# Delta-rule attention with a GELU feed-forward: the row steps of the block inversion move from VectorE to GpSimd

## The chip, the cores and the metric

The kernel runs on one core of a Trainium2 chip. The metric is the time of one execution in microseconds of the device; all times here are from runs of the kernel before the change. A core has five engines that run beside each other, each with its own queue in program order: TensorE (PE, with its weight loads PEld), VectorE (DVE), ScalarE (ACT), GpSimd (POOL) and SyncE (SP, here only for issuing DMAs).

## What is computed

Inputs are q, k, v of shape (4, 8, 768, 48), beta of shape (4, 8, 768), and two weight matrices of 384 x 2048 and 2048 x 384, all in float32.

```python
k_n = k / (norm(k) + 1e-06)
for t in range(768):                       # for each of 32 heads
    y[t] = q[t] @ state
    v_old = k_n[t] @ state
    state = state + beta[t] * outer(k_n[t], v[t] - v_old)
x = y, as 3072 tokens of 384               # (batch, time) x (head, dim)
h = x @ w_in
out = (0.5 * h * (1 + erf(h / sqrt(2)))) @ w_out
```

## The kernel before

**Attention.** The 768 steps are cut into 12 chunks of 64. A chunk of two of the four batches is a unit (`tiles[c, a]`, a = 0, 1). Inside a chunk the recurrence is a triangular system of 64 x 64 for each head. Two chunks make a group g (0 to 5) with 64 systems. Each system is split into blocks of 32: the two diagonal blocks are inverted by elimination, and the off-diagonal block is put together by two levels of small matmuls, the joins.

The parts of a group that the change touches, with their lines:

- `norms`, `prep`, `finish` (L338 to L362): sums of squares of k on ScalarE and VectorE (L354), a power on GpSimd (L356), and the factors on VectorE (L306 to L310).
- `eliminate_steps(g)` (L475): `scales` transposes the factors (L481, VectorE) and spreads them over a triangle (L486, GpSimd); `flip` transposes the diagonal blocks into `Nu`, 128 partitions x 32 x 32 (L491); `scaled_flip` multiplies by the factors (L496). Then 30 row steps follow, each needing the one before: step j multiplies column j by row j into `tmp` (L510) and adds it to the rows below (L512), (31 - j) x j elements of each partition; j = 1 and j = 30 are one instruction (L505). `diagonal` (L516) writes ones. `back` transposes the result into `XM` (L521) and `Zf` (L525); a third copy within `Zf` is ScalarE's (L529). All the rest of the list is VectorE's.
- `join_steps(g)` makes three runs of joins (L602): level 0 of the first chunk; level 1 of the first with level 0 of the second; level 1 of the second. Level 0 is evicted by VectorE (L614), level 1 by ScalarE through `put_off` and `copy_out` (L581).
- `state_steps(c)`: keys and queries against the state (L676, subtracted at L687), the solve (L711), outputs and the state's update (L741, L752; read at L757 and L767), and the turning of the outputs into tokens (L803).
- `scale_v` (L381) on GpSimd scales each V as it arrives.

**Feed-forward.** Each layer is multiplied by seven products in place of eight. From chunk 4 on, the layers run over pairs of chunks. The first layer is four blocks (`part_of_layer`, L943) of eleven products; each product is two matmuls of 256 columns. VectorE first forms four differences of the tokens (`mix_x`, L908), then reads each block's PSUM at L971, L1002 (`add_p5`), L979 and L991. The second layer (`two`, L877; `read2`, L1045 to L1056) has seven products of eight matmuls for each chunk. The products of the feed-forward stand in one fixed line (`behind`).

**What sets the order.** Every step is put in a list `plan` with a position in units of chunks: `at(first, last, steps)` spreads steps between two positions, `emit` sorts all and issues them. A pair's first layer begins at w - 1 and its two layers end at w + 1, where w is the even chunk whose attention runs meanwhile. VectorE runs in the order of the plan; ScalarE has some orders kept (`keep`), TensorE some runs (`together`, `behind`), and a scheduler orders the rest, GpSimd and SP included. `rows_of(g, w, pieces)` puts the elimination's list in the plan piece by piece, each piece a number of steps with its first and last position. Before, the row steps of groups 3 to 5 are spread from w - 1.03 to w - 0.245, between VectorE's reads for the first layer.

Of the kernel before, what the change touches and what calls it, by code (L numbers as in the profile page):

```python
# [19 lines left out]
def kernel(  # L20
# [150 lines left out]
    G = Gp[0]  # L171
    spare = Gp[1].rearrange("q a f n -> q (a f n)")
    low = spare[:, 0:HB * HB].rearrange("q (a b) -> q a b", b=HB)
    early_sq = spare[:, HB * HB:HB * HB + H * D].rearrange("q (h d) -> q h d", d=D)
    nc.gpsimd.memset(mask, 1.0)
    nc.gpsimd.memset(low, 1.0)
    nc.gpsimd.affine_select(out=low, in_=low, compare_op=ALU.is_ge, fill=0.0, base=-1,
# [134 lines left out]
    def squares(u, n, engine=None):  # L312
        kd = u.Kn[:, :, 0:D]
        if engine is nc.gpsimd:
            ksq = su.tile([128, H, D], F32, tag="w_e", name="ksq")
        elif engine is None:
            if u.a == 0:
                ns["ksq"] = more[0].tile([128, NA, H, D], F32, tag="TX", name="ksq")
            u.ksq = ns["ksq"][:, u.a]
            keep(nc.scalar.activation, u.ksq, kd, ACT.Square)  # L320
            return
        else:
            ksq = early_sq
        engine.tensor_tensor(ksq, kd, kd, op=ALU.mult)
        nc.vector.tensor_reduce(n, ksq, axis=AX.X, op=ALU.add)
# [148 lines left out]

    def eliminate_steps(g):  # L475
        steps = []

        def scales():
            gt = wk.tile([128, HB], F32, tag="gt", name="gt", bufs=1)
# [13 lines left out]
                scaled_flip()  # L493

        def scaled_flip():
            nc.vector.tensor_tensor(Nus[g], Nus[g], XMs[g], op=ALU.mult)  # L496

        def eliminate(j):
            nu = Nus[g]
            n = HB - 1 - j  # L500
            if j == 1 or n == 1:
                to = (slice(2, HB), slice(0, 1)) if j == 1 else (slice(HB - 1, HB), slice(0, j))
                by = (slice(2, HB), slice(1, 2)) if j == 1 else (slice(j, j + 1), slice(0, j))
                factor = nu[:, 1, 0:1] if j == 1 else nu[:, j + 1, j:j + 1]
                nc.vector.scalar_tensor_tensor(nu[:, to[0], to[1]], nu[:, by[0], by[1]], factor,  # L505
                                               nu[:, to[0], to[1]], ALU.mult, ALU.add)
                return
            tmp = wk.tile([128, HB * HB // 4], F32, tag="tmp", name="tmp", bufs=1)
            tmp = tmp[:, 0:n * j].rearrange("q (i c) -> q i c", i=n)
            nc.vector.tensor_tensor(tmp, nu[:, j + 1:, j:j + 1].to_broadcast([128, n, j]),  # L510
                                    nu[:, j:j + 1, 0:j].to_broadcast([128, n, j]), op=ALU.mult)
            nc.vector.tensor_tensor(nu[:, j + 1:, 0:j], nu[:, j + 1:, 0:j], tmp, op=ALU.add)  # L512

        def diagonal():
            flat = Nus[g].rearrange("q i c -> q (i c)")
            nc.vector.memset(flat[:, 0:HB * HB:HB + 1], 1.0)  # L516

        def back(x):
            nu = Nus[g]
# [56 lines left out]
    def put_off(name, dst, src):  # L576
        copies[name].append((dst, src))
# [6 lines left out]
    def join_run(g, ts0, ts1):  # L584
# [21 lines left out]
        for level, u0, psJ in sets:  # L606
            for p in range(2):
                for e in range(2):
                    us = slice(u0 + e, u0 + 2 * H, 2)
                    at_ = p * C + e * HB  # L610
                    src = psJ[at_:at_ + HB, :, e * HB:(e + 1) * HB]
                    if level == 0:
                        low_ = slice(p * C + HB, (p + 1) * C)
                        nc.vector.tensor_tensor(  # L614
                            xm[low_, us, :], src,
                            gm[low_, us].unsqueeze(2).to_broadcast([HB, H, HB]), op=ALU.mult)
                    else:
                        put_off("join", zf[p * C:p * C + HB, us, HB:C], src)
# [28 lines left out]
    def join_steps(g):  # L647
        a, b = range(NA), range(NA, 2 * NA)
        return [(join_run, g, a, ()), (join_run, g, b, a), (join_run, g, (), b)]
# [440 lines left out]
    def at(first, last, steps):  # L1090

        total, done, timed = sum(s[0] for s in steps), 0.0, []
        for w, *step in steps:
            timed.append((first + (last - first) * (done + 0.5 * w) / total, step))
            done += w
        return timed
# [164 lines left out]
    for c in range(4, NC):  # L1261
        us = [tiles[c, a] for a in range(NA)]
        even = c % 2 == 0
        for name, src, t in (("Kb", k, {4: 1.8, 5: 2.73, 6: 3.25}.get(c, c - (2.8 if even else 3.45))),
                             ("Qb", q, {4: 3.2, 5: 3.9}.get(c, c - (1.2 if even else 1.24)))):
            plan += [at(t, t + 0.01, [(1.0, load_blocks, c, name, src)])]
        for name, t in (("Kn", {4: 2.1, 5: 2.74, 7: 4.57}.get(c, c - (2.1 if even else 2.62))),
                        ("Kp", {4: 3.6, 5: 4.3}.get(c, c - (0.6 if even else 0.8)))):
            plan += [at(t, t + 0.01, [(1.0, load_k, c, name)])]
        t = {4: 2.7262, 5: 2.955, 7: 4.43}.get(c, c - (2.5 if even else 2.92))  # L1270
        plan += [at(t, t + 0.0005, [(1.0, turned_k, u) for u in us])]
        t = {4: 3.88, 5: 4.45}.get(c, c - (0.25 if even else 0.9))
        plan += [at(t, t + 0.01, [(1.0, turned_q, u) for u in us])]
    def gram(c):
        return [(grams, [tiles[c, a] for a in range(NA)])] if c < NC else []
# [16 lines left out]
    def second(c, t):  # L1292

        return [at(t + x, t + x + 0.001, steps) for x, steps in (
            (0.2, [(1.0, mix, c, 3, h) for h in range(2)]), (0.42, [(1.0, read_x, c)]))]

    for c in (2, 3, *range(4, NC, 2)):
        n = FH // blocks(c)
# [7 lines left out]
        else:  # L1306
# [2 lines left out]

    plan += [at(3.19, 3.191, [(1.0, transposed, u, (1,)) for u in fourth]),  # L1310
             at(3.1, 3.101, [(1.0, together, *gram(5))]),
             at(2.93, 2.931, [(1.0, norms, 5)]), at(2.95, 2.951, [(1.0, prep, 5)]),
             at(3.11, 3.111, [(1.0, finish, 4)]),
             state_at(3, 3.367, 3.59, 3.72, 3.93, second=query(3))]
    plan += rows_of(2, 3, ((1, 0.112, 0.113), (2, 0.16, 0.2), (4, 0.224, 0.31),
                           (2, 0.325, 0.365), (1, 0.395, 0.4), (2, 0.485, 0.5),
                           (2, 0.508, 0.54), (5, 0.6, 0.685), (7, 0.76, 0.88),
                           (3, 1.0, 1.05), (5, 1.07, 1.1), (1, 1.153, 1.154),
                           (1, 1.2, 1.201), (1, 1.201, 1.202)))
    for w in range(4, NC, 2):  # L1320
        more_to_come = w + 2 < NC
        if w == 4:
            begins = 0.25, 0.33, 0.41, 0.51, 0.6, 0.66, 0.7, 0.78, 0.87, 0.945
            n6, p6, n7, p7 = 0.53, 0.56, 0.75, 0.8
        else:
            begins = -0.22, -0.1, 0.02, 0.14, 0.27, 0.38, 0.42, 0.6, 0.76, 0.93
            n6, p6, n7, p7 = 0.3, 0.34, 0.56, 0.58
            plan += rows_of(w // 2, w, ((1, *((-1.19, -1.189) if w > 6 else (-1.05, -1.049))),
                                        (1, *((-1.18, -1.179) if w > 6 else (-1.04, -1.039))),
                                        (1, -1.035, -1.034), (4, -1.03, -1.0),  # L1330
                                        (3, -1.0, -0.95), (3, -0.935, -0.855), (2, -0.843, -0.785), (1, -0.77, -0.75),
                                        (3, -0.742, -0.692), (3, -0.677, -0.597), (2, -0.585, -0.527), (1, -0.512, -0.5),
                                        (3, -0.484, -0.434), (3, -0.419, -0.339), (2, -0.327, -0.269),
                                        (2, -0.255, -0.245), (2, -0.24, -0.23)))
        begins = [w + t for t in begins]
        j0, j1, j2 = join_steps(w // 2)
        plan += [at(begins[0], begins[0] + 0.001, [(1.0, together, j0, *query(w))]),
                 at(begins[1], begins[1] + 0.001, [(1.0, together, j1, *gram(w + 2))]),
                 state_at(w, *begins[2:6], second=[j2] + gram(w + 3)),
                 state_at(w + 1, *begins[6:], second=query(w + 1))]  # L1340
        plan += spread("join", 4, begins[1] + 0.025)
        plan += spread("join", 4, begins[3] + 0.02)
        if more_to_come:
            plan += spread("gram", 2, begins[1] + 0.01) + spread("gram", 2, begins[1] + 0.05)
            plan += spread("gram", 4, begins[3] + 0.04)
            plan += [at(w + n6, w + n6 + 0.001, [(1.0, norms, w + 2)]), at(w + p6, w + p6 + 0.001, [(1.0, prep, w + 2)]),
                     at(w + n7, w + n7 + 0.001, [(1.0, norms, w + 3)]), at(w + p7, w + p7 + 0.001, [(1.0, prep, w + 3)]),
                     at(w + p7 + 0.04, w + p7 + 0.041, [(1.0, finish, w + 2)])]
# [32 lines left out]
```

## Time and profile before

| what | us |
|---|---|
| median of 3 runs | 672.28 (671.87 to 673.04) |
| the profiled execution | 671.28 |
| its span, first to last instruction | 669.5 |
| mean granted TensorE clock in it | 0.962 |
| VectorE, L512 + L510 (168 each) | 59.0 + 56.9 |
| GpSimd, power L356 (10) | 30.8 |
| GpSimd, scaling of V L381 (18) | 15.4 |
| first layer of chunks 6 and 7 begins | 388.82 |
| first layer of chunks 8 and 9 begins | 491.29 |

An instruction's line in a timeline gives its start, its length, the engine, the line in the code, what it writes and reads, and in brackets how long the engine was idle ahead of it and who ended that. A line of the waits gives the engine and line that waited, for whom, the total, how often and the longest. "x4" behind a matmul row counts matmuls and weight loads together. Matmuls overlap, so the spacing of their starts tells more than their lengths.

### The profile page before, as it was taken

To read this page: it belongs to the slowest core of one execution; us is meant where nothing else is said; L and a number is where in the kernel's file an instruction comes from. 1 tells how busy PE (TensorE), PEld (TensorE's weight loads), DVE (VectorE), ACT (ScalarE), POOL (GpSimd) and SP (SyncE) were. 2 spreads that over 40 slices of the span, in tenths; PEclk is the share of its full clock that TensorE was granted. 3 is DMA by queue.
4 is the path that set the end of the run, shared out by engine and by line. 5 is a ranking of instruction groups with operands and counts; after the bars stand their busy time and mean duration, and the time that the engine had idled before them with its cause. 6 is when DMAs were issued, how large, how long until landed. Compare 5 with 4: busy or idle time off the path is not lost.

```text
span 669.5 us, 20804 instructions
## 1 busy us (share of the span) xinstructions
PE 621.9 (93%) x8998; PEld 551.8 (82%) x8998; DVE 490.1 (73%) x991; ACT 258.6 (39%) x584; POOL 68.1 (10%) x62
## 2 busy tenths in 40 slices
PE   5778999998998999869899989899989899999997
PEld 4667877766998899858799978799978799998997
DVE  7999989997779975689856689866689866333431
ACT  3576778333530365214461124362114441133300
POOL 4053002002200001300001310001210000000000
PEclk9578999999899999979999989999999999999999
DMA  9886682104333404431214520305120100010010
GB/s 130 176 254 181 105 222 63 24 12 80 49 60 46 72 10 72 80 60 18 32 23 82 90 49 12 38 14 98 31 55 0 25 4 14 14 24 1 0 25 24
DMA packets 158429, 39.70 MB, mean 59 GB/s; under 512 B 150017, under 2 KB 153217, under 8 KB 158337
## 3 DMA queue, kind: packets, MB, share of 16 engines
q1 hardware_dynamic: 155664, 37.34, 29.1%
q10 hardware_dynamic: 2672, 1.03, 0.8%
q8 instruction: 70, 1.15, 0.7%
q14 instruction: 23, 0.18, 0.1%
HBM read 33.62 MB, written 4.72 MB: 57 GB/s over the span
## 4 chain that ended last, share of the span: by engine, by line
PE 62%; DVE 25%; issue 6%; ACT 3%; DMA 1%; POOL 1%; SPq 0%; DVEq 0%; ACTq 0%; POOLq 0%
PE psX L877 10%; PE psY L943 8%; PE psY L877 7%; PE psX L943 5%; PE psV L943 4%; DVE tmp L510 4%; DVE Nu L512 4%; PE psG L419 4%; PE psV L877 3%; PE psZ L877 3%; PE psZ L943 3%; PE psO L844 2%; PE psK L676 2%; PE psH L826 2%; PE psT L398 2%
## 5 line engine op out<-in xcount | busy, mean ns | idle before, releaser
L943 PE MATMUL psX<-xT,w_in_sb 128*128 128x256 f32 (+1 forms) x288 | 63.7, 349 | 4.4 <-ACT pu L926 3.2
L512 DVE TENSOR_TENSOR Nu<-Nu,tmp 128x58 f32<-128x58 f32 (+13 forms) x168 | 59.0, 351 | 5.8
L510 DVE TENSOR_TENSOR tmp<-Nu 128x58 f32<-128x58 f32 (+13 forms) x168 | 56.9, 339 | 4.6
L356 POOL TENSOR_TENSOR n<-n,half 128x16 f32<-128x16 f32 x10 | 30.8, 3076 | 281.9 <-DVE n L354 232.1
L943 PEld LDWEIGHTS psX<-xT,w_in_sb 128*128 128x128 f32 x288 | 47.4, 191 | 11.0 <-ACT pu L926 4.4
L877 PE MATMUL psX<-w_out_sb,G 128*128 128x192 f32 x320 | 56.3, 329 | 0.0
L943 PE MATMUL psY<-xT,w_in_sb 128*128 128x256 f32 (+1 forms) x192 | 44.2, 361 | 10.9 <-DVE pu L1002 10.9
L877 PEld LDWEIGHTS psX<-w_out_sb,G 128*128 128x128 f32 x320 | 52.1, 190 | 0.5
L943 PEld LDWEIGHTS psY<-xT,w_in_sb 128*128 128x128 f32 x192 | 32.7, 196 | 16.2 <-DVE pu L1002 12.9
L826 PE MATMUL psH<-xT,w_in_sb 128*128 128x256 f32 x192 | 44.1, 383 | 1.5 <-ACT G L926 1.4
L844 PE MATMUL psO<-w_out_sb,G 128*128 128x384 f32 x128 | 43.9, 490 | 0.0
L826 PEld LDWEIGHTS psH<-xT,w_in_sb 128*128 128x128 f32 x192 | 35.8, 190 | 8.3 <-ACT G L926 2.3
L926 ACT COPY pu<-psZ 128x512 f32<-128x512 f32 x40 | 23.5, 586 | 45.2 <-PE psZ L943 23.2
L926 ACT COPY xT<-psX 128x768 f32<-128x768 f32 x9 | 7.2, 799 | 85.3 <-PE psX L803 85.3
L926 ACT ACTIVATE G<-G 128x512 f32<-128x512 f32 x40 | 25.2, 630 | 26.9 <-DVE G L979 26.5
L844 PEld LDWEIGHTS psO<-w_out_sb,G 128*128 128x128 f32 x128 | 23.6, 190 | 14.0
L1015 DVE TENSOR_TENSOR G<-G 128x512 f32<-128x512 f32 x20 | 13.6, 690 | 25.7 <-PE psX L877 25.7
L877 PE MATMUL psY<-w_out_sb,G 128*128 128x192 f32 x160 | 27.9, 327 | 2.0 <-DVE o_sb L1045 2.0
L877 PE MATMUL psV<-w_out_sb,G 128*128 128x192 f32 x160 | 28.0, 328 | 1.1 <-ACT y L688 1.1
L877 PE MATMUL psZ<-T,pu 128*128 128x192 f32 x160 | 28.4, 330 | 0.0
L877 PE MATMUL psY<-T,G 128*128 128x192 f32 x160 | 28.3, 329 | 0.0
L877 PE MATMUL psX<-T,G 128*128 128x192 f32 x160 | 28.1, 329 | 0.0
(186 smaller groups left out, 1316.8 us busy)
## 6 DMA issues: line engine op xcount, KB each, us to landing
Kp<-in_k_dram SPq DMA_DIRECT2D x76, 96.0 KB, 3.2
w_out_sb<-in_moe_w_in_dram SPq DMA_DIRECT2D x24, 256.0 KB, 4.1
w_raw<-in_moe_w_out_dram SPq DMA_DIRECT2D x16, 384.0 KB, 4.9
V<-in_v_dram SPq DMA_DIRECT2D x48, 96.0 KB, 3.2
out_dram<-o_sb SPq DMA_DIRECT2D x40, 96.0 KB, 2.2
Qp<-in_k_dram SPq DMA_DIRECT2D x64, 32.0 KB, 2.3
Qp<-in_q_dram SPq DMA_DIRECT2D x64, 32.0 KB, 2.3
Qp<-in_q_dram SPq DMA_DIRECT2D x16, 96.0 KB, 4.1
```

The source lines that it names most:

```text
L356: nc.gpsimd.tensor_tensor(flat, flat, half, op=ALU.pow)
L398: nc.tensor.transpose(psT[:, j, :], flat[:, j * 128:(j + 1) * 128], ident)
L419: nc.tensor.matmul(psG[HALF[p], r, i * NP + j, :], lhsT=u.Kt[rows, p, j, :], rhs=(u.Qt if x else u.Kt)[rows, p, j, :], start=True, stop=True)
L510: nc.vector.tensor_tensor(tmp, nu[:, j + 1:, j:j + 1].to_broadcast([128, n, j]), nu[:, j:j + 1, 0:j].to_broadcast([128, n, j]), op=ALU.mult)
L512: nc.vector.tensor_tensor(nu[:, j + 1:, 0:j], nu[:, j + 1:, 0:j], tmp, op=ALU.add)
L676: nc.tensor.matmul(u.psK[to, x, r, j, :], lhsT=(u.Qt if x else u.Kt)[rows, p, j, :], rhs=St[rows, u.a, p ^ r, j, :], start=True, stop=True)
L826: nc.tensor.matmul(psH, lhsT=w_in_sb[:, f // 2, m, f % 2 * 128:(f % 2 + 1) * 128], rhs=xTs[c][:, m, :], start=(m == 0), stop=(m == NM - 1))
L844: nc.tensor.matmul(u.psO, lhsT=G[:, u.a, f, :], rhs=w_out_sb[:, f, :], start=(f == 0), stop=(f == NF - 1))
L877: nc.tensor.matmul(ps_, lhsT=lhs[:, f, :], rhs=rhs[:, f, :], start=first and f == 0, stop=f == FH - 1, skip_group_check=not first)
L926: i = fn(*args, **kw)
L943: nc.tensor.matmul(ps_[:, i], lhsT=lhs[:, f // 2, f % 2 * 128:(f % 2 + 1) * 128], rhs=rhs, start=first and i == 0, stop=True, skip_group_c ...
L1015: nc.vector.tensor_tensor(a12, a12, a11, op=ALU.subtract)
```

## The change

- For groups 2 to 5 the scaled flip, all row steps and the diagonal's ones run on GpSimd; j = 1 and j = 30 are two instructions there. Groups 0 and 1 are left on VectorE.
- For groups 2 to 5 the three runs of joins are two: level 0 of both chunks, then level 1 of both (`join_both`); the eight evictions of each level are together.
- In the plan, the row steps are no longer spread between VectorE's reads; the transposes ahead of them, the joins and all steps of both chunks' chains, and several loads and transposes of k and q have new positions. Chunks 4 and 5 have their squares in spare storage instead of the buffer of `mix_x`.

```diff
     def eliminate_steps(g):
         steps = []
+        rows_on = nc.gpsimd if g > 1 else nc.vector
...
         def scaled_flip():
-            nc.vector.tensor_tensor(Nus[g], Nus[g], XMs[g], op=ALU.mult)
+            rows_on.tensor_tensor(Nus[g], Nus[g], XMs[g], op=ALU.mult)
...
-                nc.vector.scalar_tensor_tensor(nu[:, to[0], to[1]], nu[:, by[0], by[1]], factor,
-                                               nu[:, to[0], to[1]], ALU.mult, ALU.add)
-                return
+                if g < 2:
+                    nc.vector.scalar_tensor_tensor(nu[:, to[0], to[1]], nu[:, by[0], by[1]], factor,
+                                                   nu[:, to[0], to[1]], ALU.mult, ALU.add)
+                    return
...
-            nc.vector.tensor_tensor(tmp, nu[:, j + 1:, j:j + 1].to_broadcast([128, n, j]),
-                                    nu[:, j:j + 1, 0:j].to_broadcast([128, n, j]), op=ALU.mult)
-            nc.vector.tensor_tensor(nu[:, j + 1:, 0:j], nu[:, j + 1:, 0:j], tmp, op=ALU.add)
+            rows_on.tensor_tensor(tmp, nu[:, j + 1:, j:j + 1].to_broadcast([128, n, j]),
+                                  nu[:, j:j + 1, 0:j].to_broadcast([128, n, j]), op=ALU.mult)
+            rows_on.tensor_tensor(nu[:, j + 1:, 0:j], nu[:, j + 1:, 0:j], tmp, op=ALU.add)
...
+    def join_both(g, level):
+        xm, zf, off = XMs[g], Zf[g % 2], Gs[g]
+        gm = gms[g].rearrange("q t h -> q (t h)")
+        psJ = dn("psJ").rearrange("q b (k n) -> q b k n", n=2 * HB)
+        for cc in range(2):
+            for k in range(H):
+                for p in range(2):
+                    us = slice(2 * (cc * H + k), 2 * (cc * H + k) + 2)
+                    rows = slice(p * C + level * HB, p * C + (level + 1) * HB)
+                    nc.tensor.matmul(psJ[HALF[p], cc, k, :],
+                                     lhsT=(xm if level else off)[rows, us, :],
+                                     rhs=zf[rows, us, HB:C] if level else xm[rows, us, :],
+                                     start=True, stop=True)
...
         if w == 4:
-            begins = 0.25, 0.33, 0.41, 0.51, 0.6, 0.66, 0.7, 0.78, 0.87, 0.945
+            begins = 0.07, 0.17, 0.27, 0.4, 0.52, 0.6, 0.64, 0.73, 0.83, 0.92
...
-            begins = -0.22, -0.1, 0.02, 0.14, 0.27, 0.38, 0.42, 0.6, 0.76, 0.93
-            n6, p6, n7, p7 = 0.3, 0.34, 0.56, 0.58
+            begins = -0.27, -0.15, -0.04, 0.06, 0.18, 0.28, 0.36, 0.5, 0.66, 0.84
+            n6, p6, n7, p7 = 0.2, 0.25, 0.45, 0.5
+            plan += rows_of(w // 2, w, ((1, -1.12, -1.119), (1, -1.1, -1.099), (1, -1.09, -1.089),
+                                        (31, -1.08, -0.6), (1, -0.33, -0.329), (1, -0.325, -0.324),
+                                        (1, -0.323, -0.322)))
...
-        plan += [at(begins[0], begins[0] + 0.001, [(1.0, together, j0, *query(w))]),
-                 at(begins[1], begins[1] + 0.001, [(1.0, together, j1, *gram(w + 2))]),
-                 state_at(w, *begins[2:6], second=[j2] + gram(w + 3)),
+        plan += [at(begins[0], begins[0] + 0.001, [(1.0, together, (join_both, w // 2, 0), *query(w))]),
+                 at(begins[1], begins[1] + 0.001, [(1.0, together, (join_both, w // 2, 1), *gram(w + 2))]),
+                 state_at(w, *begins[2:6], second=gram(w + 3)),
                  state_at(w + 1, *begins[6:], second=query(w + 1))]
```

In `begins` the ten positions are the first and second run of joins, the four steps of `state_steps` of chunk w, and the four of chunk w + 1. In the queues that follow from the new plan, the transposes L521 and L525 of groups 3 to 5 stand on VectorE behind the third block's read L979; TensorE has the first run of joins after 19 of the third block's 22 matmuls; on GpSimd the two scalings of the odd chunk's V stand ahead of the row steps, one of them ahead of the scaled flip (groups 4 and 5), or within the row steps (group 3).

## The prediction

> **What bounds the kernel now.** I read the totals first, then the waits of TensorE from 178 us on (where the first changed group starts), then a table of stages, then the order of time around the worst stages, and last the few rows of GpSimd.
>
> ```profile
> PE 621.9 (93%) x8998; PEld 551.8 (82%) x8998; DVE 490.1 (73%) x991; ACT 258.6 (39%) x584; POOL 68.1 (10%) x62
> ```
>
> TensorE (PE) is busy for 93%: at most some 47 us of idle time is to be had, and only what the changed stages hold. GpSimd (POOL) is nearly empty. Who TensorE waited for after 178 us:
>
> ```profile
> PE psY L943 <- DVE pu L1002: 10.9, 5, 5.1
> PE psX L943 <- ACT pu L926: 3.2, 3, 1.1
> PE psJ L602 <- DVE XM L521: 2.6, 3, 0.9
> PE psX L803 <- DVE V L767: 2.3, 2, 1.2
> PE psY L877 <- DVE o_sb L1045: 2.0, 1, 2.0
> PE psX L943 <- DVE p L1048: 1.2, 1, 1.2
> ```
>
> Together 22.2 us, nearly all behind VectorE (DVE). The largest sits at the start of each first layer of a pair of chunks. Stages (columns: length, busy time of PE, weight loads, DVE, ACT, POOL, granted clock, DMA share, GB/s):
>
> ```profile
> 284.00:300.00 16.00, 10.90 (x40) 8.85 (x40) 14.34 (x33) 2.89 (x5) 1.66 (x2) 0.79 0.36 68
> ...
> 387.00:404.00 17.00, 14.59 (x64) 12.44 (x63) 15.35 (x40) 4.12 (x9) 1.79 (x2) 0.90 0.22 47
> 404.00:423.00 19.00, 18.54 (x85) 15.66 (x83) 17.67 (x42) 8.02 (x14) 0.00 (x0) 1.00 0.18 22
> 423.00:430.00 7.00, 5.32 (x109) 4.56 (x110) 6.90 (x10) 3.43 (x5) 0.00 (x0) 1.00 0.24 30
> ```
>
> In these stages VectorE, not TensorE, is full. The row steps (L510, L512) are what fills it, and they stand in its queue ahead of the reads of PSUM (L971, L1002) that TensorE waits for. The idle time also costs clock. In order of time, TensorE at the start of the layer of chunks 6 and 7:
>
> ```profile
> 393.14 1.03 PE L943 MATMUL psX<-xT,w_in_sb 128*128 128x256 f32 x4
> 396.57 1.50 PE L943 MATMUL psY<-xT,w_in_sb 128*128 128x256 f32 x4 [2.41 <-DVE pu L1002]
> 397.87 1.91 PE L943 MATMUL psV<-xT,Sw 128*128 128x256 f32 x4
> 399.57 1.54 PE L943 MATMUL psV<-xT,w_in_sb 128*128 128x256 f32 x4
> ```
>
> A product is normally spaced 0.865 us. Here three take 400.95 - 396.57 = 4.38 instead of 2.6 us: 1.8 lost on top of the 2.41. After the 5.10 us wait at 293.39 it is 298.45 - 293.39 - 2.6 = 2.5; after the 2.94 at 499.58, 3.51 for two, 1.8. So these starts cost 10.9 + 6.1 = **17.0 us**. The Trainium skill (TensorE: Matmul & The Clock Gate, section "HAM oscillation — how this bites in real kernels") gives no PE-idle gap over some 3.4 us as the rule; by it the gaps of 2.41 and 2.94 would be free of a clock loss and the starts worth 3.6 less, but the rows show the loss, so I count it.
>
> **The change, part by part.** T is the start of a pair's first layer (388.82 above).
>
> *Row steps off VectorE.* One group has 28 pairs L510/L512 of 0.339 and 0.351, some 19.3 us, plus the flip's product 1.2 and two L505: 21 us, four groups, 84 us less for VectorE. Only TensorE's waits count. The three starts lose their 17.0. Groups 3 to 5 start there; group 2 starts at 180 and clogs VectorE until 228, so the 2.0 (L1045) and 1.2 (L1048) go too: **-3.2**. The 2.3 at the turning (L803 <- L767) came because the state's reads stood behind `factors`, which waited 3.02 us for GpSimd's power; the new order has the reads ahead: **-2.3**.
>
> *Rows on GpSimd.* No row here shows such a small product on GpSimd. What it shows:
>
> ```profile
> 14.06 1.91 POOL L484 TENSOR_TENSOR XM<-G,gt 128x1024 f32<-128x1024 f32 x1 [7.17 <-DVE gt L481]
> ...
> 40.66 4.96 POOL L458 TENSOR_TENSOR P<-P,mask 128x512 f32<-128x512 f32 x4
> ...
> 220.54 0.83 POOL L381 TENSOR_TENSOR V<-V,n 128x384 f32<-128x384 f32 x1 [41.55 <-DMA V<-in_v_dram]
> ```
>
> From 384 to 1024 elements, (1.91 - 0.83) / 640 = 1.69 ns an element. L458, whose two operands are both read in full, takes 1.24 each, with 0.15 fixed 2.1 ns. Fixed part: two L381 in a row take 1.61, 0.80 apart, less 384 x 1.69 = 0.15; five memsets of 128 elements in 0.78 bound it below at 0.05; a chained one (each step now waits for the step before it) may add 0.05, so 0.2 above. A group has 60 instructions (j = 1 and j = 30 are two each now) with 2 x 4960 = 9920 elements. Low: 60 x 0.05 + 9920 x 1.09 (the slope of the one-operand selects, 0.29 for 128 and 1.27 for 1024 elements) = 13.8 us. High: 60 x 0.2 + 4960 x (1.69 + 2.1) = 30.8. I take 60 x 0.1 + 9920 x 1.69 = **22.8**: the products' slope, since the broadcast operand is as in L381 and L484, and a fixed part halfway between memset and L381.
>
> What does it have to meet? The last L1048 group ends 1.3 us after the product before the last (T - 2.6), then the flip (1.93) ends near T + 0.8; the scaled flip on GpSimd (1.91) T + 2.75; a scaling of V that stands between it and the rows 0.83, T + 3.6. Rows until T + 26.4, transposed (L521) 2.1, with 0.2 of hand-over **T + 28.7**. TensorE gets to the first join after 2 blocks and 19 of 22 matmuls of the third, each 0.4325: T + 26.9, or 27.4 with what the start still loses. So it waits 1.3 us, three times **+3.9**; the 2.6 of L602 <- L521 that it replaces go (**-2.6**). Group 2 has 38 us from 182 to T = 220 and needs no more than 31: nothing. The 3.2 behind ScalarE (pu L926) come from its two copies of Zf (2.1 us) standing ahead of pu, and these still do: unchanged.
>
> *The shared start.* Rows on GpSimd do not run freely beside VectorE. L512 at 392.23 took 0.78 instead of 0.27, while a scaling of V ran on GpSimd (392.01 to 392.89); the first L908 at 281.78 took 1.17 instead of 0.43 and ended with GpSimd's select; reads of PSUM at the same time (L971 at 395.03, 0.69) were not slowed. So VectorE's operations with two SBUF operands wait for the GpSimd instruction in progress. In the first layer only the four of `mix_x` (L908) are such; they meet the scaled flip, and the second is needed for P6 at T + 1.7 and comes at about T + 3.1: 1.4, rounded to 1.5, three times **+4.5**. Beside group 2's rows some ten such (L693, L1010, L1011, L1015) lose up to 0.4 each, 4 us; VectorE's 20 freed us hide it, and without that cover it is 4.
>
> *Joins in two runs.* 64 matmuls as before, and eight evictions L614 of 0.42 in one go instead of two times four. They stand ahead of L455 and L991 now (3.4 + 1.2 us), behind which P3 of the fourth block waits; that comes some 10 us after the join, so 0, and at worst the 1.7 of four evictions per group.
>
> *Begun sooner.* The chains' positions are 0.1 to 0.2 units sooner at turning, which moves six matmuls of turning ahead of one product. V of the odd chunk is loaded after the turning: its four DMAs on SP then stand ahead of the outputs for the later groups. Loads of Kb and Qb a little sooner in the same queue: 0 (DMA engines 20 to 50% busy). Squares of chunks 4 and 5 in spare storage: 0, at best the 1.0 that VectorE waited at 165.
>
> **Sum**: -17.0 + 4.5 - 3.2 - 2.3 - 2.6 + 3.9 = -16.7. The profiled execution took 671.28, so 654.6; the median shown is 1.0 above it, so **655.6**.
>
> **Rivals.**
> - *GpSimd late, slower than before.* At the high price the rows end at T + 34.4, the join is ready at 36.7, TensorE waits 9 us and loses 1.8 of clock: 10.8 x 3 = 32.4 instead of 3.9, **684**. For it: L458's 2.1 ns, and that TensorE has no other work ahead of the join in its queue. It decides from a group's price of about 26.5 us (a wait of 5 and the clock, 16.7 in all). The Trainium skill speaks against the change here (GPSIMD Engine Reference, section "Elementwise — side-by-side cycle accounting"): 2.6 cycles an element for two inputs, at 1.2 GHz an estimate of 2.17 ns; with a fixed 0.1 that is 27.5 a group and no change in time. The rows of L381 and L484 lie below it.
> - *V late or engines in each other's way, faster by less.* In before, the odd chunk's scalings of V ran at T + 3.2 and T + 6.1 (392.01, 394.89), as their DMAs landed; the rows now stand behind them in order. If they still come at T + 6.1, rows begin at 6.9, 3.3 later: +3.3 x 3, **666**. For it: 72.1 us of GpSimd waiting for V in the waits. Against: the earlier turning.
> - *GpSimd early.* At 20 us or less the join never waits, and mix_x slips in before the scaled flip: 655.6 - 3.9 - 4.5, **647**.
>
> **Chances.** Forecast 0.45 (649 to 661), early 0.13, V or contention 0.15, GpSimd near break-even 0.05 (no change), late 0.22. Range 645 to 679: leaves out half of the early case's lower end and the later part of the late one. Faster by over 0.2% (about what can be told from no change) 0.73, within it 0.05, slower 0.22.
>
> **What would show it.** Right: psY <- pu at the layers' starts falls from 10.9 to below 4 and the clock there stays at 1.00; DVE busy falls by some 80 us, POOL rises to 160 to 190; a pair of chunks takes 97 to 99 us instead of 102.5. Wrong: L521 on VectorE waits for GpSimd for over 5 us per group (rows dearer than 26 us, or begun late), and psJ waits take the place of psY's. It would also be wrong if VectorE's PSUM reads become longer while rows run.

## The result, and the profile after

The changed kernel takes **703.08 us** (median of 4 runs, 701.89 to 703.66); the kernel before, run beside it, 672.08 (669.66 to 673.04). The ratio is 1.0465, 95% interval 1.0434 to 1.0496: slower, where 655.6 was forecast. The profiled execution of the changed kernel has a span of 699.9 us (before: 669.5) and a mean granted clock of 0.949 (before: 0.962).

From the page of the changed kernel: the totals, the engines' shares of the chain that ended last, and the two groups of row steps with the group of joins (columns: busy, mean ns of one, idle time ahead).

```profile
PE 632.7 (90%) x8998; PEld 563.6 (81%) x8998; DVE 418.2 (60%) x751; ACT 260.4 (37%) x584; POOL 201.4 (29%) x310
...
PE 56%; POOL 20%; DVE 14%; issue 4%; ACT 3%; DMA 2%; SPq 0%; POOLq 0%; DVEq 0%; ACTq 0%
...
L518 POOL TENSOR_TENSOR Nu<-Nu,tmp 128x30 f32<-128x30 f32 (+14 forms) x120 | 63.8, 532 | 9.1
...
L636 PE MATMUL psJ<-XM,G 32*64 32x64 f32 x256 | 13.1, 288 | 37.0 <-DVE XM L527 37.0
```

VectorE gave up 71.9 us, somewhat less than the 80 that were meant, and GpSimd took 133.3. But GpSimd, which held 1% of the chain of waits before, now holds 20%, and TensorE stood idle 37.0 us ahead of the joins. In the waits of TensorE from 178 us on and, last, of VectorE:

```profile
PE psJ L636 <- DVE XM L527: 37.0, 4, 11.9
PE psY L977 <- DVE TX L942: 4.3, 3, 1.5
...
PE psZ L977 <- DVE TX L942: 1.0, 1, 1.0
PE psX L837 <- DVE V L801: 0.8, 1, 0.8
...
DVE XM L527 <- POOL Nu L518: 35.0, 4, 11.2
```

The psY <- pu line that led the list before is gone altogether. In its place stands one line, and the last line shows who is behind it: the transpose L527 on VectorE only passes on a wait for GpSimd's last row step. The waits from 178 us on, without psJ <- L527 (before: L521), fell from 20.7 to 7.8 us; psJ rose from 2.6 to 37.0; TensorE's busy time, which grows when its clock is lowered, rose by 10.8. Together that is -12.9 + 34.4 + 10.8 = 32.3, against 30.4 in the span.

Group 4 shows it in order of time (its pair's first layer begins at T = 396.42). GpSimd's timeline:

```profile
397.31 2.37 POOL L501 TENSOR_TENSOR Nu<-Nu,XM 128x1024 f32<-128x1024 f32 x1 [1.67 <-DVE Nu L496]
399.64 1.01 POOL L385 TENSOR_TENSOR V<-V,n 128x384 f32<-128x384 f32 x1
400.61 0.43 POOL L516 TENSOR_TENSOR tmp<-Nu 128x30 f32<-128x30 f32 x1
...
435.01 0.24 POOL L516 TENSOR_TENSOR tmp<-Nu 128x30 f32<-128x30 f32 x1
435.32 0.25 POOL L518 TENSOR_TENSOR Nu<-Nu,tmp 128x30 f32<-128x30 f32 x1
```

From 400.61 to 435.57 the 60 row instructions take 35.0 us. Look at the two last: 30 elements take 0.24 us, and the next begins 0.07 after the end. TensorE's timeline, and then its stages (length, busy time, granted clock, DMA share, GB/s):

```profile
437.67 3.68 PE L636 MATMUL psJ<-XM,G 32*64 32x64 f32 x64 [11.86 <-DVE XM L527]
```

```profile
425.00:438.00 13.00, 1.14 (x10) 0.61 0.00 0
438.00:445.00 7.00, 7.00 (x132) 0.50 0.26 35
445.00:455.00 10.00, 10.00 (x160) 1.00 0.17 21
```

After the stop TensorE works on for 7.3 us at half clock (437.67 to 444.98), so about 3.7 us of work are lost beside the wait itself. After the stops of groups 3 and 5 it is longer:

```profile
322.58:332.34 9.76, 9.76 (x138) 0.50 0.25 30
551.50:561.03 9.53, 9.53 (x138) 0.50 0.25 31
```

After group 2's short stop (2.71 us up to 220.71) the clock is 0.50 from 223.11 to 226.52 alone.

### The profile page after: what moved, and what is told of

Its sections match the earlier page's. It is cut to its first block, busy times and chain, and to the rows that moved or that the text cites. A ratio compares the mean times of both kernels' runs of the same rounds, so it can differ in the third digit from the quotient of the medians.

```text
span 699.9 us, 20832 instructions
## 1 busy us (share of the span) xinstructions
PE 632.7 (90%) x8998; PEld 563.6 (81%) x8998; DVE 418.2 (60%) x751; ACT 260.4 (37%) x584; POOL 201.4 (29%) x310
## 4 chain that ended last, share of the span: by engine, by line
PE 56%; POOL 20%; DVE 14%; issue 4%; ACT 3%; DMA 2%; SPq 0%; POOLq 0%; DVEq 0%; ACTq 0%
PE psX L911 10%; POOL Nu L518 9%; POOL tmp L516 9%; PE psY L911 6%; PE psY L977 5%; PE psG L423 4%; PE psX L977 3%; PE psZ L911 3%; PE psK L710 3%; PE psJ L636 3%; PE psO L878 2%; PE psV L911 2%; PE psZ L977 2%; PE psV L977 2%; PE psH L860 2%
## 5 line engine op out<-in xcount | busy, mean ns | idle before, releaser
L518 POOL TENSOR_TENSOR Nu<-Nu,tmp 128x30 f32<-128x30 f32 (+14 forms) x120 | 63.8, 532 | 9.1
L977 PE MATMUL psX<-xT,w_in_sb 128*128 128x256 f32 (+1 forms) x288 | 65.5, 359 | 0.0
L516 POOL TENSOR_TENSOR tmp<-Nu 128x30 f32<-128x30 f32 (+14 forms) x120 | 60.3, 503 | 9.1
L977 PEld LDWEIGHTS psX<-xT,w_in_sb 128*128 128x128 f32 x288 | 50.5, 200 | 6.0
L636 PE MATMUL psJ<-XM,G 32*64 32x64 f32 x256 | 13.1, 288 | 37.0 <-DVE XM L527 37.0
L860 PEld LDWEIGHTS psH<-xT,w_in_sb 128*128 128x128 f32 x192 | 35.7, 190 | 9.8 <-ACT G L960 2.3
L636 PEld LDWEIGHTS psJ<-XM,G 32*64 32x64 f32 x256 | 12.4, 199 | 38.3 <-DVE XM L527 35.5
L1005 DVE TENSOR_TENSOR psY<-psY,pu 128x512 f32<-128x512 f32 x20 | 14.0, 699 | 46.0 <-PE psY L977 45.0
L1013 DVE TENSOR_TENSOR G<-psY,pu 128x512 f32<-128x512 f32 x20 | 13.8, 689 | 42.4 <-PE psY L977 38.2
L878 PEld LDWEIGHTS psO<-w_out_sb,G 128*128 128x128 f32 x128 | 23.6, 190 | 14.0
L527 DVE STREAM_TRANSPOSE XM<-Nu 128x1024 f32<-128x1024 f32 x6 | 12.2, 2032 | 35.0 <-POOL Nu L518 35.0
L535 ACT COPY Zf<-Zf 32x1024 f32<-32x1024 f32 x10 | 10.4, 1044 | 54.5 <-DVE Zf L531 54.3
```

The lines of the kernel that those rows point to most:

```text
L516: rows_on.tensor_tensor(tmp, nu[:, j + 1:, j:j + 1].to_broadcast([128, n, j]), nu[:, j:j + 1, 0:j].to_broadcast([128, n, j]), op=ALU.mult)
L518: rows_on.tensor_tensor(nu[:, j + 1:, 0:j], nu[:, j + 1:, 0:j], tmp, op=ALU.add)
L636: nc.tensor.matmul(psJ[HALF[p], cc, k, :], lhsT=(xm if level else off)[rows, us, :], rhs=zf[rows, us, HB:C] if level else xm[rows, us, :], ...
L860: nc.tensor.matmul(psH, lhsT=w_in_sb[:, f // 2, m, f % 2 * 128:(f % 2 + 1) * 128], rhs=xTs[c][:, m, :], start=(m == 0), stop=(m == NM - 1))
L878: nc.tensor.matmul(u.psO, lhsT=G[:, u.a, f, :], rhs=w_out_sb[:, f, :], start=(f == 0), stop=(f == NF - 1))
L977: nc.tensor.matmul(ps_[:, i], lhsT=lhs[:, f // 2, f % 2 * 128:(f % 2 + 1) * 128], rhs=rhs, start=first and i == 0, stop=True, skip_group_c ...
```

## The experiments

**Theory 1**: GpSimd's chain of dependent steps ends after TensorE has reached the first join; the wait and the half clock behind it are the loss, and nothing else in the change is. Rivals: the joins in two runs or the chains begun sooner are the loss; or GpSimd and VectorE hold each other up. Each run was timed beside the kernel before; the ratio is to that one.

### Same steps, tiny operands (e4)

```diff
+            if g > 1:
+                n = j = 1
+                tmp = tmp[:, 0:1, 0:1]
-            rows_on.tensor_tensor(tmp, nu[:, j + 1:, j:j + 1]...
+            rows_on.tensor_tensor(tmp, nu[:, j + 1:j + 1 + n, j:j + 1]...
...
-            rows_on.tensor_tensor(nu[:, j + 1:, 0:j], ...
+            rows_on.tensor_tensor(nu[:, j + 1:j + 1 + n, 0:j], ...
```

> The changed kernel with the same 60 row instructions a group on GpSimd from group 2 on, each cut to one element of a partition, so that the blocks' inversion is left out in these groups. Theory 1 in the form that each chained instruction has a fixed 0.27 us (0.19 busy and 0.08 gap): the 60 take 16 us a group, the join waits go, 648 to 662 us. With the prediction's fixed 0.10 the 60 would take 6 us, with the same time of the kernel. Rival (the joins' form or order is the loss): above 690 us.

Measured: **657.9 us** (654.14 to 658.28), ratio 0.9772 [0.9728, 0.9816]. The groups of this kernel's GpSimd (busy, mean ns | idle ahead):

```profile
L519 POOL TENSOR_TENSOR tmp<-Nu 128x1 f32<-128x1 f32 x120 | 24.8, 206 | 9.2
L521 POOL TENSOR_TENSOR Nu<-Nu,tmp 128x1 f32<-128x1 f32 x120 | 24.3, 202 | 9.0
```

One element costs 0.204 us, and 18.2 / 240 = 0.076 lie between a step and the one that needs it: 0.280 fixed, 16.8 us a group before any element is counted. The rest of group 4's 35.0 us, 18.2 for 9920 elements, makes 1.83 ns an element. psJ <- L527 falls to 2.1 us. Everything else of the change is still in this kernel, so neither the joins' form nor the earlier chains are a loss by themselves.

### Rows back on VectorE (e1)

```diff
-        rows_on = nc.gpsimd if g > 1 else nc.vector
+        rows_on = nc.vector
...
-                if g < 2:
+                if True:
```

> All row steps back on VectorE, everything else of the change kept (joins in two runs, earlier starts, new order). Theory 1 (GpSimd's chain of 60 dependent steps, 35 us a group, ends after TensorE reaches the first join): the chain shrinks to about 60 x 0.35 = 21 us, the join waits psJ <- XM fall from 37.0 us to under 6, VectorE's busy time rises by about 72 us and takes back a part of the starts' gain: 660 to 676 us. Rival (joins in two runs, or the earlier starts, are themselves the loss): the time stays above 690.

Measured: 701.71 us (697.7 to 704.76), ratio 1.0433 [1.0378, 1.0488]. TensorE's waits from 178 us on:

```profile
PE psY L977 <- DVE G L1013: 14.2, 6, 5.3
PE psY L977 <- DVE pu L1036: 10.2, 6, 2.6
PE psZ L977 <- DVE TX L942: 7.7, 3, 3.2
PE psJ L636 <- DVE XM L527: 2.3, 3, 0.8
```

The join wait went as theory 1 has it, but the time missed its 660 to 676: 32.1 us of waits for VectorE's reads took its place. The change's plan packs the row steps into 0.48 of a unit, in front of those reads; it presupposes a VectorE without rows. By its time alone this run would speak for the rival; e4 and e8 speak against it.

### Only the rows moved, in the old plan (e2), and only the joins changed (e8)

e2 is the kernel before with `rows_on = nc.gpsimd if g > 1 else nc.vector` in the scaled flip, the row steps and the diagonal. e8 is the kernel before with

```diff
-        plan += [at(begins[0], ..., [(1.0, together, j0, *query(w))]),
-                 at(begins[1], ..., [(1.0, together, j1, *gram(w + 2))]),
-                 state_at(w, *begins[2:6], second=[j2] + gram(w + 3)),
+        plan += [at(begins[0], ..., [(1.0, together, (join_both, w // 2, 0), *query(w))]),
+                 at(begins[1], ..., [(1.0, together, (join_both, w // 2, 1), *gram(w + 2))]),
+                 state_at(w, *begins[2:6], second=gram(w + 3)),
```

> The kernel before with only the row steps, the scaled flip and the diagonal moved to GpSimd from group 2 on; its own plan and its three join runs stay. Theory 1: the first join waits 8 to 12 us in groups 3 to 5 here too, while the psY <- pu waits shrink as VectorE is freed: 685 to 705 us. Rival (the new order makes the rows late, not GpSimd): join waits under 3 us a group and 655 to 668 us.

> The kernel before with only its joins put in two runs of 32 + 32 matmuls in place of three runs; rows on VectorE, plan as it was. The prediction's term (0, at worst 1.7 us a group): 670 to 677 us. Rival (one join run of both chunks makes TensorE wait for the eight read-outs between the levels): over 679 us, with psJ waits above 3 us a group.

e2: 681.35 us (680.76 to 681.89), ratio 1.0133 [1.0096, 1.017], which is 3.7 us under the 685 to 705 of theory 1. Of its waits (over the whole span, 0.7 us of it ahead of 178 us):

```profile
PE psJ L604 <- DVE XM L523: 29.5, 4, 13.0
```

The same wait without the new order: 13.0, 7.9 and 7.9 us in groups 3 to 5, and none in group 2. psY <- pu is gone here too. So late rows alone, in the old plan, cost about 9 us, and the changed kernel lies 21.7 us above e2 with the same instructions on GpSimd. The two traces show where: in the changed kernel the join waits from 178 us on add to 37.0 us instead of 28.8, TensorE waits 5.3 us for `mix_x` instead of not at all, and its busy time is 7.5 us longer (632.7 against 625.2). The new plan thus makes late rows dearer, and theory 1's "nothing else in the change" holds only where the rows are in time, as in e4. e8: 671.76 us, ratio 0.9996 [0.9978, 1.0013], with 2.7 us of psJ <- L521: the joins in two runs cost nothing and bring nothing.

### Rows sooner, or joins later (e3, e7)

```diff
 e3
-            plan += rows_of(w // 2, w, ((1, -1.12, -1.119), ... (31, -1.08, -0.6),
+            s = 0.3 if w > 6 else 0.03
+            plan += rows_of(w // 2, w, ((1, -1.12 - s, -1.119 - s), ... (31, -1.08 - s, -0.6 - s),
 e7
-            begins = -0.27, -0.15, -0.04, 0.06, 0.18, 0.28, 0.36, 0.5, 0.66, 0.84
+            begins = -0.06, 0.02, 0.09, 0.17, 0.26, 0.34, 0.4, 0.53, 0.68, 0.85
-                                        ... (1, -0.33, -0.329), (1, -0.325, -0.324), (1, -0.323, -0.322)
+                                        ... (1, -0.12, -0.119), (1, -0.115, -0.114), (1, -0.113, -0.112)
```

> The changed kernel with the scales, the flip, the scaled flip and the row steps 0.3 of a plan unit earlier in groups 4 and 5 (some 17 us), 0.03 earlier in group 3, where the factors aren't there sooner. Theory 1: the rows still take about 35 us a group but end before TensorE reaches the join in groups 4 and 5: their waits fall from 11.9 and 11.8 us to under 1, group 3 keeps 8 to 10 of its 10.6: 703 - 2 x (11.8 + about 3 of clock) = 670 to 678 us. Rival (GpSimd and VectorE hold each other up, so that rows put beside more of VectorE's work stretch): rows over 42 us, waits of 5 us and more stay, over 688 us.

> The changed kernel with its rows where they are, but the joins of groups 3 to 5 set 0.2 of a plan unit (some 11 us) later, and the first chunk's steps after them closed up. Theory 1: the join waits fall from 11 us to under 3 a group and the time by 3 x (11 + 3 of clock), to 661 to 670 us. Rival (the joins have to stand early, since the chunks' chains must be done before the next pair's first layer): waits of psX, psU, psG or of the next pair's start take their place, above 680 us.

e3: 678.56 us (675.4 to 679.57), ratio 1.0083 [1.0049, 1.0117]. e7: 680.09 (679.34 to 680.71), ratio 1.0129 [1.0106, 1.0153]. Their psJ waits, 17.2 in e3 (first line) and 16.4 in e7:

```profile
PE psJ L636 <- DVE XM L527: 17.2, 4, 9.8
```

```profile
PE psJ L636 <- DVE XM L527: 16.4, 4, 4.9
```

Both moved the time by over 20 us with nothing of the work changed, which speaks for theory 1 and against rows that stretch beside VectorE (35.7 us for group 4's in e3, from 389.70 to 425.36). The 680.09 of e7 lies in the range of its rival, but the waits that the rival names did not come: the largest new one is 0.9 us (psY <- diag). The two runs ended 0.6 (e3) and 10 us (e7) above what was expected, since 2.3 us (e3, groups 4 and 5) and 4.4 to 4.9 us (e7, groups 3 to 5) of each wait were left, and the half clock after these shorter stops lasted about as long as after the long ones. e3's group 4 stopped for 2.31 us up to 427.49; its stages of TensorE:

```profile
429.00:436.00 7.00, 6.73 (x94) 0.53 0.26 33
436.00:440.00 4.00, 4.00 (x73) 0.96 0.38 45
```

### The scaled flip alone back on VectorE (e11)

```diff
-            rows_on.tensor_tensor(Nus[g], Nus[g], XMs[g], op=ALU.mult)
+            nc.vector.tensor_tensor(Nus[g], Nus[g], XMs[g], op=ALU.mult)
```

> The changed kernel with the scaled flip alone back on VectorE, the row steps still on GpSimd. Theory 1: the rows start 1.1 us sooner in each group (1.23 against 2.37 us), so psJ <- XM falls from 37.0 to 32 to 34 us, and mix_x no longer stands beside a scaled flip on GpSimd, which takes 2 of the 4.3 + 1.0 us of psY and psZ <- TX: 694 to 700 us. Rival (VectorE and GpSimd never hold each other up, and the psY <- TX wait has another cause): the second operation of mix_x still takes over 2 us.

Measured: 696.59 us (695.71 to 699.74), ratio 1.0377 [1.0346, 1.0409]. psJ falls to 33.4, as expected. In the changed kernel the second operation of `mix_x` ran beside GpSimd's flip (397.31 to 399.68):

```profile
397.51 2.46 DVE L942 TENSOR_TENSOR TX<-xT,TX 128x256 f32<-128x256 f32 x1
```

In e11 it takes 0.42 (second line):

```profile
396.60 0.42 DVE L942 TENSOR_TENSOR TX<-xT 128x256 f32<-128x256 f32 x1
397.05 0.42 DVE L942 TENSOR_TENSOR TX<-xT,TX 128x256 f32<-128x256 f32 x1
```

So the two engines do hold each other up there. But TensorE waits 5.3 us for TX as before, now all in psZ: VectorE's own flip, 1.23 us, stands ahead of `mix_x` instead. That part of the expectation missed.

### All groups sooner (e5, e9)

e5 goes on from e3: for group 3 the factors come 0.16 of a unit sooner and for groups 4 and 5 0.04, the rows follow, the joins stand 0.03 to 0.05 later. Its keys of chunk 7 are loaded into the buffer of chunk 6's before the norms of chunk 6 have read it, which changes group 3's factors but no instruction's size. e9 mends that:

```diff
 e9 against the changed kernel
-    7: 4.57}                                        # load of Kn
+    7: 4.455}
-            begins = 0.07, 0.17, 0.27, 0.4, ...     # w == 4
-            n6, p6, n7, p7 = 0.53, 0.56, 0.75, 0.8
+            begins = 0.12, 0.2, 0.28, 0.4, ...
+            n6, p6, n7, p7 = 0.45, 0.56, 0.61, 0.65
-            begins = -0.27, -0.15, -0.04, 0.06, ... # w > 4
-            n6, p6, n7, p7 = 0.2, 0.25, 0.45, 0.5
+            begins = -0.24, -0.12, -0.03, 0.06, ...
+            n6, p6, n7, p7 = 0.2, 0.25, 0.42, 0.46
+            s = 0.34 if w > 6 else 0.15             # rows sooner by s, as in e3
-                           (1, 1.02, 1.021), (1, 1.03, 1.031), (1, 1.031, 1.032)
+                           (1, 1.02, 1.021), (1, 1.03, 1.031), (1, 1.1, 1.101)
```

> The rows of the run before begun sooner still: the factors of group 3 stand 0.16 and of groups 4 and 5 0.04 of a plan unit earlier, the row steps follow them, and the joins stand 0.03 (groups 3 to 5) and 0.05 (group 2) of a unit later. Theory 1 (only the end of GpSimd's chain against the join counts): the 17.2 us that were left of psJ <- XM fall under 4, no other wait takes their place, 654 to 662 us, so faster than the kernel before. Rival (GpSimd and VectorE hold each other up beside the starts, or the factors taken sooner cost the starts what the joins win): 667 us or more, with psY <- pu or psX waits in place of psJ.

> The early rows with three places of the run before mended: the keys of chunk 7 are loaded after the norms of chunk 6 have read the same buffer (in that run they were not, so its group 3 had other factors), the copies of the inverse's top on ScalarE stand behind a read-out for TensorE that they had held up (6.3 us of psZ <- pu), and group 3's flip stands behind the masked products that it had held up (3.7 us of psY <- P). Theory 1: the 6.3 and 3.7 us go, psJ <- XM stays under 3 us in all: 650 to 657 us. Rival (each thing put sooner only pushes the next one back): 661 us or more, with new waits of 8 us and more.

e5: 663.26 us (662.21 to 664.52), ratio 0.988 [0.9855, 0.9905], 1.3 us above what theory 1 gave; psJ 0.9 us, but two new waits:

```profile
PE psZ L977 <- ACT pu L960: 6.3, 1, 6.3
PE psY L775 <- DVE P L459: 3.9, 2, 3.7
```

The first: ScalarE held `pu` behind its copies of Zf, which waited for the rows of group 2. The second: group 3's flip stood ahead of the masked products on VectorE. Here the rival had a point; e9 gives each another place in the plan. e9: **656.42 us** (655.34 to 658.25), ratio 0.9778 [0.9754, 0.9802], clock 0.98. Its largest waits from 178 us on:

```profile
PE psJ L636 <- DVE XM L527: 6.8, 4, 5.3
PE psK L710 <- ACT Zf L587: 1.8, 3, 0.8
```

psJ was to stay under 3; 5.3 of the 6.8 are group 3's, whose flip had to go behind the masked products.

### The old plan with early rows (e10, e12)

Is the rest of the change needed? e10 is e2 with the rows put sooner. It missed its 652 to 660: in groups 4 and 5 they already followed the flip directly, and the flip the factors, so only group 3 moved. e12 takes the norms of the odd chunk sooner:

```diff
 e12 against e10
-    c - (2.1 if even else 2.62)                     # load of Kn
+    c - (2.1 if even else 2.69)
-            n6, p6, n7, p7 = 0.3, 0.34, 0.56, 0.58
-            s = 0.11 if w > 6 else 0.07
+            n6, p6, n7, p7 = 0.3, 0.34, 0.45, 0.48
+            s = 0.31 if w > 6 else 0.07
-                     at(w + p7 + 0.04, ..., [(1.0, finish, w + 2)])
+                     at(w + p7 + (0.124 if w > 4 else 0.04), ..., [(1.0, finish, w + 2)])
```

> The kernel before with its own plan and three join runs, rows on GpSimd from group 2 on, and the scaled flip and the rows begun sooner: 0.11 to 0.13 of a plan unit (some 7 us) in groups 4 and 5, 0.07 to 0.1 (some 5 us) in group 3. It tells whether the joins in two runs and the earlier chains of the change are needed for a gain. Theory 1 (they aren't; only GpSimd's end against the join counts, at the wait and half of the 6.7 us of half clock behind it): of the 29.5 us of psJ <- XM 8 to 11 are left, two of three slow-clock stretches go, 681 - 20 - 2 x 3.3 = 652 to 660 us. Rival (the old plan's late chains keep their waits when VectorE is free): 664 us or more, with psY <- pu and psX <- V waits as in the kernel before.

> The run before (old plan, three join runs, rows on GpSimd) moved its row steps in group 3 alone: in groups 4 and 5 they already followed the flip directly, and the flip stood behind the factors. Here the norms of the odd chunk are taken sooner, so that flip and rows of groups 4 and 5 begin some 8 us earlier. Theory 1 (only GpSimd's end against the join counts): of the 15.6 us of psJ <- XM 2 to 5 are left (group 3 keeps 2.3), two of the slow-clock stretches of some 3.3 us go, the psX <- V wait of 3.9 us stays: 648 to 658 us. Rival (the change's other parts, two join runs and earlier chains, are needed for a gain of this size): 662 us or more, with psX <- V and psY waits of 8 us and more.

e10: 671.69 us, ratio 1.0002 [0.9986, 1.0018]; group 3's wait fell from 13.0 to 2.3, 15.6 in all were left. Its time lies in the rival's range; e12 is what decides between the two. e12: **655.31 us** (653.9 to 657.81), ratio 0.9748 [0.9721, 0.9776]. Its largest waits:

```profile
PE psX L805 <- DVE V L769: 4.3, 2, 3.3
PE psJ L604 <- DVE XM L523: 3.7, 3, 2.7
```

With rows on GpSimd in time, the old plan with three runs of joins is no slower than the new one: the intervals of e9 and e12 overlap. Both kernels are faster than before and after.

## Why the prediction was wrong, step by step

**The step that failed** is "I take 60 x 0.1 + 9920 x 1.69 = 22.8". Measured: 60 x 0.280 + 9920 x 1.83 = 35.0. The fixed part is 10.8 of the missing 12.2 us. It was taken from two scalings of V in a row, which do not need each other, and from memsets; no row of before showed a small GpSimd product that waits for the one before it. (Its memsets of one element, L1365, took 0.10 each, so the 0.05 as a lower bound was too low by rows that were there.) The 0.2 given as an upper bound was therefore none, and with it neither the 30.8 nor the 679 at the range's end. The element's price lay between the two slopes that were read (1.69 and 2.1) and was a small miss. The page that the prediction weighed, the Trainium skill's GPSIMD Engine Reference (section "Elementwise — side-by-side cycle accounting"), has 2.6 cycles an element, from which the prediction worked out an estimate of 2.17 ns. The measured 1.83 lies below it, and it was not the element that decided.

In group 4, by T:

| | predicted | measured |
|---|---|---|
| scaled flip ends | T + 2.75 | T + 3.3 |
| rows begin | T + 3.6 | T + 4.2 |
| rows end | T + 26.4 | T + 39.2 |
| TensorE at the join | T + 27.4 | T + 29.4 |
| join ready | T + 28.7 | T + 41.2 |
| wait | 1.3 | 11.9 |

The prediction counted 1.5 us at T for `mix_x` but let TensorE arrive at the join only 0.5 late; with all 1.5 its wait would have been 0.3, not 1.3. That is small beside the 12.8 us by which the rows ended late.

**The rival "GpSimd late" had the mechanism right and its price too low.** Put the measured waits of groups 3 to 5 into its sum, 10.6 + 11.9 + 11.8 = 34.3, and half of the 26.6 us at half clock behind them, 13.3: 47.6 instead of 3.9 gives 699.3. The rest is **group 2, costed at nothing**: it has 38 us of room, and its rows took 37.9 (180.64 to 218.5). TensorE waited 2.7 us and then ran 3.4 us at half clock, so 4.4 in all: 703.7, against 703.08 measured. That it comes out so closely is partly luck, since the errors of the other terms below nearly cancel (+2.5 for `mix_x`, +0.8 for the turning, -3.2 for ScalarE).

The other steps:

- *The starts, -17.0*: right. No psY <- pu is left in the changed kernel, nor the 2.0 and 1.2 of group 2. e4, which keeps all but the rows' length, is 14.8 us below the kernel before beside it (672.74); the prediction's terms without its 3.9 for the join, and with the 2.1 of psJ that e4 still has, make -18.5.
- *The turning, -2.3*: 0.8 us are left of it (psX <- V L801), so -1.5.
- *mix_x beside the scaled flip, +4.5*: about right in size, 4.3 + 1.0 us of waits, and 1.7 more for the clock, which was 0.50 behind group 3's (284.61 to 287.96). Right in cause, since e11 takes the collision away (2.46 to 0.42).
- *Joins in two runs, 0*: right (e8).
- *The 3.2 behind ScalarE, unchanged*: wrong, none are left in the changed kernel and 0.2 in e4. Why was not tried; e5 shows with 6.3 us that the order of Zf's copies and `pu` on ScalarE can cost this and more.
- *V late or engines in each other's way*: V did not come late (394.81 and 399.64, T - 1.6 and T + 3.2). VectorE slowed some rows, where its operations with two SBUF operands ran: in group 2 a step of 238 elements took 0.98 us at 197.10 beside two of them, in group 4 0.66 at 416.25 beside a read of PSUM.
- *What would show it right*: psY <- pu went from 10.9 to nothing. VectorE's busy time fell by 71.9 us, not some 80; `mix_x` grew from 9.7 to 16.8 us. GpSimd rose to 201.4, past the 160 to 190, and a pair of chunks took 113.9 us (396.42 to 510.30) instead of 97 to 99; in e9, with the rows in time, it takes 98.0 (382.33 to 480.32).
- *What would show it wrong*: "L521 on VectorE waits for GpSimd for over 5 us per group" and "psJ waits take the place of psY's". These are the last and the first line of the waits above.

## What to carry to other kernels

Before a chain of small dependent instructions moves to another engine, price it by the chain: instructions times (shortest busy time + hand-over), and only then the elements; a price read from instructions that do not wait for each other is no bound on it. Then look at when the chain can begin, not only at how much time the new engine has free: here the changed kernel, whose rows of some 35 us a group begin with the pair's first layer, is 31 us slower than before, and e9, where they begin some 15 us sooner, is 15 us faster (group 4's at T + 4.2 and T - 10.9; e9's plan differs from the changed one in a few other places too). And count a stop of TensorE as the wait plus the slow clock that may follow: behind the joins of the changed kernel 3.4 to 9.8 us at half speed.

## What the hardware showed that was not expected

- A float32 product on GpSimd of one element on 128 partitions takes 0.204 us, and a dependent one begins 0.076 us after it (means of 240 in e4).
- TensorE's clock falls to 0.50 behind stops much shorter than the join waits, and the length of a stop does not decide it. In the changed kernel a stop of 1.45 us up to 284.61 was followed by 0.50 until 287.96, one of the same length up to 400.11 by 1.00. In the kernel before, 1.73 us up to 167.26 were followed by 0.50 from 168.50 to 171.92, and 2.03 us up to 213.26 by 1.00. In e11, 2.36 us up to 283.21 left it at 1.00; in e3, 2.31 us up to 427.49 were followed by 0.50 from 429.46 to 436.29. The Trainium skill's "HAM oscillation — how this bites in real kernels" (TensorE: Matmul & The Clock Gate) has some 3.4 us of idle time as the limit; in these runs shorter stops were enough at times. What decides between the two outcomes was not tried.
- The time at half clock does not follow the length of the stop closely: 3.4 us after 2.71 (group 2 of the changed kernel), 6.8 after 2.31 (e3), 7.6 after 5.30 (e9), 7.3 to 9.8 after 10.6 to 11.9 (groups 3 to 5 of the changed kernel).
- So 10.4 us more of join waits in e3 than in e9 came with 23.6 us more of span (677.2 against 653.6): TensorE's busy time differs by 13.7, at a mean clock of 0.956 against 0.980.
- Beside a long GpSimd product, VectorE's operations with two SBUF operands ended only with it or after it: the `mix_x` operation above (2.46 instead of 0.42), and in e5 two of L1049, about 1.4 us elsewhere, which took 3.39 beside the scaled flip at 277.57, and the flip 2.62 instead of 2.36.
